# Experts in pairs of 256 tokens with one load of weights, and the leftovers in tiles of 32 tokens that are stationary in column groups

## The chip, the core and the metric

The kernel runs on one core of one Trainium2 chip, everything in float32 as far as the results go. The metric is device time in microseconds of one execution, the median of a few runs. A profiled execution gives the trace; its times are counted from the first instruction.

## What is computed

An attention block turns x and a small state into 8 batches of 544 rows of 512 (4352 tokens). A mixture of experts follows: each token goes to one expert, either the best by its logits or the one of the token before it, and is sent through that expert's two matrices.

```python
for b in range(B):                      # B = 8
    prev_e = -1
    for s in range(S):                  # S = 544
        fresh_e = int(np.argmax(logits[b, s]))
        if s == 0 or local_gate[b, s] < 0.5:
            e = fresh_e
        else:
            e = prev_e if prev_e >= 0 else fresh_e
        prev_e = e
        ...
        h = np.maximum(x[b, s] @ w1[e], 0.0)      # 512 -> 1024
        out[b, s] = p[e] * (h @ w2[e])            # 1024 -> 512
```

There are 8 experts, w1 is 512 x 1024 and w2 1024 x 512 for each, 4.19 MB together.

## The kernel before, in words

**Attention** (classes Attention and Batch) goes over the 8 batches in an order written out by hand and writes the token rows to `rows` in DRAM. Three of its groups of matmuls matter below, since they use parts of TensorE's array: `state_reads` (L404) has a stationary tile of 32 columns in each of four column groups (the trace calls the shape 128*32), `scores` (L336) has 64*32, and `turn` (L391) uses the whole array.

**Routing** (`Routing.route`) sorts the tokens by expert without a loop over tokens. `exc` (L580) has the running count of each expert; from its last column come the number of blocks of 128 of each expert (`nblk`) and where they end (`end`, L588). `at` is the slot of every token: count within the expert plus the expert's first slot (L600 to L611). One comparison and one small matmul (`past`, `be`) tell the expert of every block, which SP needs for the addresses of the weights. `inb`, `bc` and 40 matmuls (L656) then turn slots into lists: `slots.tok` (the token in each place of each block), `slots.row` (the same by quarter rows of 128 numbers) and, later and inside block 0, `slots.prob`. `keep(n)` issues matmuls whose result nobody reads.

**Experts** (`experts`) runs over blocks k of 128 tokens of one expert. `gather(k)` (L724) fetches quarter rows with four indirect DMAs on GpSimd's queue, `turned(k)` (L738) transposes them on VectorE into `x_t`; block 0 is gathered as whole rows (`first`, L719) and transposed on TensorE (L735). `load(k)` (L753) issues the four 1 MB loads of the weights on SP's queue, two halves of w1 into `a`, two of w2 into `c`, each double buffered by the parity of k. In block 0 the halves of `a` are loaded in quarters of 256 KB and pieces of 2 KB (L751). A block is, on TensorE, 32 matmuls with the weights stationary and the 128 tokens moving (L767), and 8 with the tokens' hidden values stationary and 512 columns of w2 moving (L774). ScalarE takes the relu (L769), VectorE scales by the probability (L776), and an indirect DMA scatters to `out` (L777). At its start block k issues the loads and the transposes of block k+1 and the gather of block k+2.

The order of the instructions on each engine is that of the code. SP waits in order: a load stands until the matmuls that read its buffer are done, and the loads behind it stand too. 41 blocks are written down; the first 34 always run, and from then on the code tests the number of blocks (`last`, L797), so that it stops after as many as the counts ask for.

Of the kernel before, what the change touches and what calls it, by code (L numbers as in the profile page):

```python
# [18 lines left out]
P = 128  # L19
# [13 lines left out]
NBLK = NT // P + E - 1  # L33
NJ = NT // P
OFF = 8192
LOW = 32
SQ = 32
CG = 4
NG = COLS // CG
Q = P // SQ  # L40
# [15 lines left out]
):  # L56

# [47 lines left out]
class Slots:  # L105


    def __init__(self, pool):

        self.tok = pool.tile([P, NBLK], I32, name="tok")  # L110

        self.row = pool.tile([P, NBLK, Q], I32, name="row")

        self.prob = pool.tile([P, NBLK], F32, name="prob")

        self.expert = pool.tile([1, 1], I32, name="expert")
        self.again = pool.tile([1, 1], I32, name="again")
        self.experts = pool.tile([1, NBLK - 1], I32, name="experts")
        self.number = pool.tile([1, 1], I32, name="number")
# [326 lines left out]
class Routing:  # L446
# [79 lines left out]
    def route(self, bank, ctx, lt, slots):  # L526
# [31 lines left out]
        for i in range(SC):  # L558
# [22 lines left out]
                                     tot.rearrange("p e c -> p (e c)"), 0.0, Alu.mult, Alu.add)  # L581
        ni = rt.tile([P, E], I32, name="ni")
        nc.vector.tensor_scalar(ni, exc[:, :, COLS], float(P - 1), None, Alu.add)
        nc.vector.tensor_scalar(ni, ni, 7, None, Alu.logical_shift_right)
        nblk = rt.tile([P, E], F32, name="nblk")
        nc.vector.tensor_copy(nblk, ni)
        end = rt.tile([P, 1, E], F32, name="end")
        nc.vector.tensor_tensor_scan(end[:, 0], on[:, 0, 1:E + 1], nblk, 0.0, Alu.mult, Alu.add)  # L588
        first = rt.tile([P, E, 1], F32, name="first")
        firstf = first.rearrange("p e o -> p (e o)")  # L590
        nc.vector.tensor_tensor(firstf, end[:, 0], nblk, op=Alu.subtract)
        nc.vector.tensor_scalar(firstf, firstf, float(P), None, Alu.mult)


        nc.scalar.copy(slots.number, end[0:1, 0, E - 1:E])
        ends = bank(E, 1)
        nc.tensor.matmul(ends, lhsT=end[0:1, 0, :], rhs=one, start=True, stop=True)
        end8 = rt.tile([E, 1], F32, name="end8")
        nc.scalar.copy(end8, ends)
        nc.vector.tensor_tensor(at, exc[:, :, :COLS], pre, op=Alu.add)  # L600
        past = rt.tile([E, NBLK], BF16, name="past")
        nc.vector.tensor_scalar(past, iof[:E, :NBLK], end8, None, Alu.is_ge)
        be = bank(1, NBLK)
        nc.tensor.matmul(be, lhsT=ones[:E - 1, 0:1], rhs=past[:E - 1], start=True, stop=True)
        nc.scalar.copy(slots.expert, be[:, :1])
        others = rt.tile([1, NBLK - 1], F32, name="others")
        nc.scalar.copy(others, be[:, 1:])
        keep(16)

        nc.vector.tensor_tensor(at, at, first.to_broadcast([P, E, COLS]), op=Alu.add)  # L610
# [75 lines left out]
        def probabilities():  # L686
# [10 lines left out]
            for d in (1, 2):  # L697
                nc.vector.tensor_tensor(slots.prob, slots.prob, prob[:, d], op=Alu.add)
            yield
# [4 lines left out]
def experts(ctx, tc, bank, w1, w2, rows, slots, route, out):  # L704
# [7 lines left out]
    xts_ = [fx.tile([P, KT, P], F32, name=f"xt{i}") for i in range(2)]  # L712
    xgs_ = [fx.tile([P, Q, KT, SQ], F32, name=f"xg{i}") for i in range(2)]

    first = fx.tile([P, D], F32, name="first")

    def gather(k):
        if k == 0:
            nc.gpsimd.indirect_dma_start(out=first, out_offset=None,  # L719
                                         in_=rows.rearrange("n q x -> n (q x)"),  # L720
                                         in_offset=bass.IndirectOffsetOnAxis(ap=slots.tok[:, :1], axis=0))
            return
        for i in range(Q):
            nc.gpsimd.indirect_dma_start(out=xgs_[k % 2][:, i].rearrange("p k t -> p (k t)"), out_offset=None,  # L724
                                         in_=rows.rearrange("n q x -> (n q) x"),
                                         in_offset=bass.IndirectOffsetOnAxis(ap=slots.row[:, k, i:i + 1], axis=0))

    def turned(k):
        if k == 0:

            for h, copy in enumerate((nc.vector.tensor_copy, nc.scalar.copy)):
                t = bank(P, KT * P // 2)
                for j in range(KT // 2):
                    q = slice((2 * h + j) * P, (2 * h + j + 1) * P)
                    nc.tensor.transpose(t[:, j * P:j * P + P], first[:, q], route.ident)  # L735
                copy(xts_[0][:, 2 * h:2 * h + 2, :], t.rearrange("p (k t) -> p k t", k=KT // 2))
            return
        nc.vector.transpose(xts_[k % 2].rearrange("p k (i t) -> p k i t", i=Q),  # L738
                            xgs_[k % 2].rearrange("p i k t -> p k i t"))

    def load(k, parts=range(4)):
        expert = slots.experts[0:1, k - 1:k] if k else slots.expert if 0 in parts else slots.again
        e = nc.values_load(expert, engines=[ET.SP], min_val=0, max_val=E - 1,
# [11 lines left out]
    def block(k, ahead=True):  # L755
        a, c, x_t = as_[k % 2], cs_[k % 2], xts_[k % 2]
        if ahead:
            load(k + 1)
            turned(k + 1)
# [77 lines left out]
```

## Time and profile before

| | |
|---|---|
| runs | 670.43 us median of 3 (670.23 to 671.66) |
| the profiled execution, its own time | 669.64 us |
| its span, first to last instruction | 667.8 us |
| attention and routing, to the first expert matmul | 119.3 us |
| expert stage, first matmul to the end of the last | 119.3 to 656.7 us |
| TensorE busy | 630.1 us, 94% of the span |
| mean granted TensorE clock | 0.985 |
| bytes moved by DMA | 206.06 MB |

Where a row of the profile names a group, it has the line, the engine, the operation, what it writes and reads, the shape (128*32 is a part of the array of 128 rows and 32 columns; 128x512 the moving data), the count, busy time and the mean length of one. A matmul's length reaches from its start to the end of its last result, and several are under way at a time; its price in a stream is the distance between starts. A timeline row has the start, the length until the last of the merged instructions ends, and the count; a bracket gives idle time before it and what ended that.

### The profile page before, as it was taken

Reading aid. Unit: us, or ns where it says so; the run is one execution under the profiler, and the core shown is the slowest. Engines: PE = TensorE matmul, PEld = TensorE weight load, DVE = VectorE, ACT = ScalarE, POOL = GpSimd, SP = SyncE. Lnnn points to the kernel's source line nnn. Section 1 sums busy time; section 2 is a strip of 40 time slices with the busy share of each in tenths; the row PEclk is TensorE's granted clock in tenths of the full one; section 3 lists DMA queues with packets and bytes.
Section 4 is the critical chain, followed back from the end, with each engine's and each line's share of the span. In section 5 each row is a group of like instructions: output and inputs, shape, how many; then the busy total and the mean of one; then the engine's idle time right before and its main releaser. Section 6 shows DMA issues by size and latency. Waiting matters only on the chain. (4 is left out here: it accounts for less than half of the span.)

```text
span 667.8 us, 10490 instructions
## 1 busy us (share of the span) xinstructions
PE 630.1 (94%) x4226; PEld 447.2 (67%) x4229; DVE 149.5 (22%) x303; ACT 98.2 (15%) x189; POOL 224.9 (34%) x226
## 2 busy tenths in 40 slices
PE   7688777999999999999999999999999999999993
PEld 2455544867777667776677766777667777667771
DVE  4798978301100001000010000100001100011000
ACT  5455422000010000101001010010100011000110
POOL 4343411522443223432234422344222443223410
PEclk9889997999999999999999999999999999999998
DMA  8969536899999999999999999998999999989910
GB/s 327 373 223 345 213 133 131 325 416 412 348 330 337 323 348 348 337 328 327 350 333 329 337 325 354 338 341 321 322 350 350 338 321 334 335 342 323 336 37 6
DMA packets 41607, 206.06 MB, mean 309 GB/s; under 512 B 9105, under 2 KB 9233, under 8 KB 21330
## 3 DMA queue, kind: packets, MB, share of 16 engines
q1 hardware_dynamic: 33570, 186.18, 75.8%
q0 software_dynamic: 7984, 19.15, 9.1%
q8 instruction: 37, 0.61, 0.4%
q14 instruction: 16, 0.13, 0.1%
HBM read 187.47 MB, written 18.88 MB: 309 GB/s over the span
## 5 line engine op out<-in xcount | busy, mean ns | idle before, releaser
L767 PEld LDWEIGHTS ps<-xt,a 128*128 128x128 f32 x2432 | 277.5, 192 | 18.2 <-issue 17.7
L767 PE MATMUL ps<-xt,a 128*128 128x128 f32 x2432 | 277.8, 275 | 0.3 <-DVE again L688 0.3
L774 PE MATMUL ps<-c,h 128*128 128x512 f32 x608 | 267.2, 592 | 0.0
L774 PEld LDWEIGHTS ps<-c,h 128*128 128x128 f32 x608 | 112.6, 190 | 127.2 <-issue 127.2
L724 POOL DMA_INDIRECT xg<-rows,row x152 | 147.2, 968 | 46.3 <-issue 46.0
L777 POOL DMA_INDIRECT out_dram<-y,tok x38 | 38.5, 1013 | 311.2 <-DVE y L776 311.2
L776 DVE TENSOR_SCALAR y<-ps,prob 128x512 f32<-128x512 f32 x38 | 28.5, 750 | 474.7 <-PE ps L774 474.7
L769 ACT ACTIVATE h<-ps 128x512 f32<-128x512 f32 x76 | 45.4, 597 | 485.6 <-PE ps L767 485.6
L428 PE MATMUL v<-sd,a 128*128 128x265 f32 x128 | 36.9, 428 | 11.6 <-ACT xr L431 8.1
L428 PEld LDWEIGHTS v<-sd,a 128*128 128x128 f32 x128 | 24.2, 203 | 22.9 <-ACT xr L431 13.6
L738 DVE STREAM_TRANSPOSE xt<-xg 128x512 f32<-128x512 f32 x37 | 25.9, 701 | 6.2 <-DMA xg<-rows,row 6.2
L379 POOL TENSOR_TENSOR e<-e,z 128x1024 f32<-128x1024 f32 x8 | 15.3, 1913 | 28.2 <-DVE z L378 28.2
L367 POOL TENSOR_TENSOR e<-e,m 128x1024 f32<-128x1024 f32 x8 | 15.3, 1913 | 16.3 <-DVE m L366 16.3
L336 PE MATMUL s<-x_t,sttc 64*32 64x512 f32 x128 | 11.2, 606 | 2.7 <-issue 2.1
L535 PE MATMUL idle<-place,identb 128*128 128x512 bf16 x42 | 12.4, 451 | 0.6 <-DVE xr L431 0.5
L431 DVE COPY xr<-v 128x530 f32<-128x530 f32 x16 | 10.9, 679 | 4.7 <-PE v L428 4.7
L391 PEld LDWEIGHTS t<-ident,e 128*128 128x128 f32 x64 | 7.5, 149 | 6.4 <-DVE m L366 3.4
L350 ACT ACTIVATE e<-s,nb 128x512 f32<-128x512 f32 x16 | 11.1, 695 | 3.5 <-DVE e L361 1.8
L371 ACT ACTIVATE e<-e 128x1024 f32<-128x1024 f32 x8 | 8.5, 1056 | 17.7 <-POOL e L367 17.7
L346 DVE TENSOR_REDUCE nb<-s 128x1 f32<-128x512 f32 x16 | 10.7, 670 | 0.6 <-PE s L336 0.6
L361 DVE STREAM_TRANSPOSE e<-s 128x512 f32<-128x512 f32 x16 | 10.4, 689 | 2.0 <-PE s L336 1.9
L391 PE MATMUL t<-ident,e 128*128 128x128 f32 x64 | 9.9, 298 | 0.8 <-DVE lt L441 0.7
(149 smaller groups left out, 181.9 us busy)
## 6 DMA issues: line engine op xcount, KB each, us to landing
c<-in_w_dram SPq DMA_DIRECT2D x76, 1024.0 KB
a<-in_w_dram SPq DMA_DIRECT2D x74, 1024.0 KB
x_t<-in_xt_dram SPq DMA_DIRECT2D x16, 512.0 KB
x_n<-in_xn_dram SPq DMA_DIRECT2D x8, 1024.0 KB
rows<-xr SPq DMA_DIRECT2D x8, 1024.0 KB
xg<-rows,row POOLq DMA_INDIRECT x152
a<-in_w_dram SPq DMA_DIRECT2D x8, 256.0 KB
out_dram<-y,tok POOLq DMA_INDIRECT x38
```

The lines of the kernel that those rows point to most:

```text
L367: nc.gpsimd.tensor_tensor(e1, e1, m1.to_broadcast([P, A, N]), op=Alu.subtract)
L379: nc.gpsimd.tensor_tensor(e1, e1, z1.to_broadcast([P, A, N]), op=Alu.mult)
L391: nc.tensor.transpose(self.t[u][:, c * P:c * P + P], self.e2[:, u, c * P:c * P + P], at.ident)
L428: nc.tensor.matmul(v[:, u, :VW], lhsT=self.a[:, u, c * P:c * P + P], rhs=at.sd[:, b, u * VW:(u + 1) * VW], start=True, stop=True)
L535: nc.tensor.matmul(idle, lhsT=identb, rhs=place.rearrange("p k c -> p (k c)"), start=True, stop=True)
L724: nc.gpsimd.indirect_dma_start(out=xgs_[k % 2][:, i].rearrange("p k t -> p (k t)"), out_offset=None, in_=rows.rearrange("n q x -> (n q) x" ...
L738: nc.vector.transpose(xts_[k % 2].rearrange("p k (i t) -> p k i t", i=Q), xgs_[k % 2].rearrange("p i k t -> p k i t"))
L767: nc.tensor.matmul(hps[:, i * P:i * P + P], lhsT=a[half][:, j, i * P:i * P + P], rhs=x_t[:, j, :], start=(j == 0), stop=(j == KT - 1))
L769: nc.scalar.activation(h[:, half * 4:half * 4 + 4, :].rearrange("p m t -> p (m t)"), hps, Act.Relu)
L774: nc.tensor.matmul(yps, lhsT=h[:, m, :], rhs=c[m // 4][:, m % 4, :], start=(m == 0), stop=(m == FK - 1))
L776: nc.vector.tensor_scalar(y, yps, slots.prob[:, k:k + 1], None, Alu.mult)
L777: nc.gpsimd.indirect_dma_start(out=out, out_offset=bass.IndirectOffsetOnAxis(ap=slots.tok[:, k:k + 1], axis=0), in_=y, in_offset=None, bou ...
```

## The change

A unit is now a **pair**: 256 tokens of one expert with one load of its weights (`pair(u)`). An expert has as many pairs as its count holds whole 256s. What is left over goes into **tiles** of 32 tokens (`class Tile`), each with a load of its expert's weights into buffers of their own (`at_`, `ct_`, single).

- In a pair the first product moves 256 columns per matmul; the second is twice the old one, one per 128 tokens. Pair 0 keeps the old shape for the first product.
- In a tile the tokens are stationary. `one()` puts the same 32 columns into each of the four column groups, and each group multiplies another quarter of the hidden values (16 matmuls, 256 columns moving). The relu is taken by ScalarE, and VectorE transposes the result in squares of 32. `two()` does the same with w2 (32 matmuls, 128 columns). The output goes out by quarter rows.
- Tile u is worked in pair u: `one()` behind the pair's first product, `two()` behind its second. When `one()` is issued, SP gets the load of the next tile's w1 (pieces of 2 KB) and GpSimd the tile's gather; behind `two()` come the load of w2 and the tile's transpose.
- 17 pairs and 63 tiles are written down; ten pairs with ten tiles always run, later pairs by a test of their number, later tiles, alone, by a test of theirs.
- The routing counts pairs and tiles, has two ends per expert and a `jump` for the tokens past the last whole pair, and 50 columns of slots instead of 41. The probabilities of the tiles are brought into quarters by four more matmuls (`probq`).

The core of the diff:

```diff
+PAIR = 2 * P
+NP = NT // PAIR
+NPMIN = NP - E * (PAIR - 1) // PAIR
+NTILE = (NT - NPMIN * PAIR) // SQ + E - 1
+NB = NP * 2
+NBLK = NB + (NTILE + Q - 1) // Q
...
+        nc.vector.tensor_copy(ni, count)
+        nc.vector.tensor_scalar(ni, ni, 8, None, Alu.logical_shift_right)
...
+        nc.vector.scalar_tensor_tensor(left, pairs, -float(PAIR), count, Alu.mult, Alu.add)
+        nc.vector.tensor_scalar(ni, left, float(SQ - 1), None, Alu.add)
+        nc.vector.tensor_scalar(ni, ni, 5, None, Alu.logical_shift_right)
...
-        nc.vector.tensor_tensor(at, at, first.to_broadcast([P, E, COLS]), op=Alu.add)
+        nc.vector.tensor_tensor(at, at, each_column(less), op=Alu.add)
+        more = rt.tile([P, E, COLS], F32, name="more")
+        nc.vector.scalar_tensor_tensor(more, at, 0.0, each_column(jump), Alu.is_ge, Alu.mult)
+        nc.vector.tensor_tensor(at, at, each_column(behind), op=Alu.add)
+        nc.vector.tensor_tensor(at, at, more, op=Alu.add)
...
+    class Tile:
...
+        def load(self, of):
+            e = index(slots.experts[0:1, NP - 1 + self.i:NP + self.i])
+            for half in range(2):
+                if of == 0:
+                    w = w1[bass.ds(e, 1), half].rearrange("o p (k f) -> (o p) k f", k=KT)
+                    nc.sync.dma_start(out=at_[:, :, half * F // 2:(half + 1) * F // 2], in_=w)
+                else:
+                    to = ct_[:, half * FK // 2:(half + 1) * FK // 2, :].rearrange("p m d -> p (m d)")
+                    nc.sync.dma_start(out=to, in_=w2[bass.ds(e, 1), half].rearrange("o p x -> (o p) x"))
...
+        def one(self):
+            hps = bank(P, FK * SQ)
+            a = at_.rearrange("p k (m g x) -> p k m g x", g=Q, x=SQ)
+            for j in range(KT):
+                for g in range(Q):
+                    nc.tensor.matmul(hps[SQ * g:SQ * g + SQ, :], lhsT=self.x_t[:, j, :], rhs=a[:, j, :, g],
+                                     start=(j == 0), stop=(j == KT - 1))
...
+        def two(self):
+            yps = bank(P, P)
+            for m in range(FK):
+                for g in range(Q):
+                    nc.tensor.matmul(yps[SQ * g:SQ * g + SQ, :], lhsT=self.h[:, m, :], rhs=ct_[:, m, g * P:g * P + P],
+                                     start=(m == 0), stop=(m == FK - 1))
...
+    def pair(u, ahead=True, tile=None, after=None):
...
+            for n in range(4):
+                hps = bank()
+                for i in range(2):
+                    f = (2 * n + i) % 4 * P
+                    for j in range(KT):
+                        nc.tensor.matmul(hps[:, i * PAIR:(i + 1) * PAIR], lhsT=a[n // 2][:, j, f:f + P],
+                                         rhs=x_t[:, j, :], start=(j == 0), stop=(j == KT - 1))
+                nc.scalar.activation(h[:, 2 * n:2 * n + 2, :].rearrange("p m t -> p (m t)"), hps, Act.Relu)
...
+        if tile:
+            tile.one()
...
+        if after:
+            after.load(0)
+            after.gather()
+        for b in range(2):
+            yps = bank()
+            for m in range(FK):
+                nc.tensor.matmul(yps, lhsT=h[:, m, b * P:b * P + P], rhs=c[m // 4][:, m % 4, :],
+                                 start=(m == 0), stop=(m == FK - 1))
...
+        if tile:
+            tile.two()
+        if after:
+            after.load(1)
+            after.turned()
...
+    gather(0)
+    tiles[0].gather()
+    gather(1)
+    turned(0)
+    tiles[0].turned()
+    next(route.probabilities)
+    load(0, range(2, 4))
+    for of in range(2):
+        tiles[0].load(of)
...
+    for u in range(NPMIN - 1):
+        pair(u, True, tiles[u], tiles[u + 1])
```

How the instructions stand, first on TensorE in the middle of the expert stage, two blocks before (`xt`, `a` and `c` are the buffers named above, the numbers tell the two of each apart):

```order
L767 MATMUL ps<-xt_1471,a_1464 128x128 x16
L767 MATMUL ps<-xt_1471,a_1465 128x128 x16
L774 MATMUL ps<-c_1468,h 128x512 x4
L774 MATMUL ps<-c_1469,h 128x512 x4
L767 MATMUL ps<-xt_1470,a_1462 128x128 x16
L767 MATMUL ps<-xt_1470,a_1463 128x128 x16
L774 MATMUL ps<-c_1466,h 128x512 x4
L774 MATMUL ps<-c_1467,h 128x512 x4
```

and one pair with its tile now (`xtt` and `htt` are the tile's tokens and hidden values, `at` and `ct` its weights):

```order
L875 MATMUL ps<-xt_1494,a_1484 128x256 x16
L875 MATMUL ps<-xt_1494,a_1485 128x256 x16
L838 MATMUL ps<-at,xtt_1498 32x256 x16
L902 MATMUL ps<-c_1488,h 128x512 x4
L902 MATMUL ps<-c_1489,h 128x512 x4
L902 MATMUL ps<-c_1488,h 128x512 x4
L902 MATMUL ps<-c_1489,h 128x512 x4
L850 MATMUL ps<-ct,htt 32x128 x32
```

The 64 matmuls of the two first products became 32 of twice the width, and the tile's two products stand behind the pair's.

SP's queue in the same place, the loads of one pair and of the tile's two halves behind them:

```order
L807 DMA a_1484<-in_w_dram 128x2048
L807 ISA
L807 DMA a_1485<-in_w_dram 128x2048
L807 ISA
L807 DMA c_1488<-in_w_dram 128x2048
L807 ISA
L807 DMA c_1489<-in_w_dram 128x2048
L794 TENSOR_LOAD experts
L827 ISA
L827 DMA at<-in_w_dram 128x4x512
L827 ISA
L827 DMA at<-in_w_dram 128x4x512
```

Before, only loads of `a` and `c` stood in it; now each pair's four are followed by two of the tile's w1 and, behind those, two of its w2.

VectorE in the routing, between the counts and the slots, before:

```order
L588 SCALAR_TENSOR_TENSOR end<-on,nblk 128x8
L591 TENSOR_TENSOR first<-end,nblk 128x8
L592 TENSOR_SCALAR first<-first 128x8
L600 TENSOR_TENSOR at<-exc,ps 128x320
L602 TENSOR_SCALAR past<-iof,end_1311 8x41
L610 TENSOR_TENSOR at<-at,first 128x320
L611 TENSOR_TENSOR at<-at,oh 128x320
```

and now, from the second `end` on:

```order
L607 SCALAR_TENSOR_TENSOR end<-on,tiles 128x8
L618 SCALAR_TENSOR_TENSOR jump<-end,tiles 128x8
L619 SCALAR_TENSOR_TENSOR jump<-jump,behind 128x8
L621 TENSOR_TENSOR at<-exc,ps 128x320
L624 TENSOR_SCALAR past<-iof,end_1321 8x17
L625 TENSOR_SCALAR past<-iof,end_1321 8x63
L637 TENSOR_TENSOR at<-at,less 128x320
L639 SCALAR_TENSOR_TENSOR more<-at,jump 128x320
L640 TENSOR_TENSOR at<-at,behind 128x320
L641 TENSOR_TENSOR at<-at,more 128x320
L642 TENSOR_TENSOR at<-at,oh 128x320
```

Three more operations on 320 columns stand there, and five more on 8 columns above them.

More of the change, by code (lines that the diff above doesn't have):

```diff
@@ L800, in last, with rest @@
         with another.Else():
-            block(k, False)
-    last(NJ - 1)
+            pair(u, False, *with_tile)
+    last(NPMIN - 1, tiles[NPMIN - 1], tiles[NPMIN])
+    def rest(i):
+        with tc.If(more > i):
+            tiles[i].one()
+            if i + 1 < NTILE:
+                tiles[i + 1].load(0)
+                tiles[i + 1].gather()
+            tiles[i].two()
+            if i + 1 < NTILE:
+                tiles[i + 1].load(1)
+                tiles[i + 1].turned()
+                rest(i + 1)
```

223 lines of the change are left out of this document (138 added, 85 removed).

## The prediction

> **What bounds the kernel now.** I read the page first, for the groups that hold TensorE's time. Columns: line, engine, operation, names and shapes, count, then busy us and mean ns of one, then idle time before.
>
> ```profile
> span 667.8 us, 10490 instructions
> ...
> L767 PE MATMUL ps<-xt,a 128*128 128x128 f32 x2432 | 277.8, 275 | 0.3 <-DVE again L688 0.3
> L774 PE MATMUL ps<-c,h 128*128 128x512 f32 x608 | 267.2, 592 | 0.0
> ```
>
> The expert stage is these two lines, and TensorE is never kept waiting in them. 608 records at 16 a block are 38 blocks. (The program has 32 + 8 matmuls in a block, the trace 64 + 16: each is recorded twice.) Next TensorE's timeline over two late blocks; columns are start, length, engine, line, operation, count.
>
> ```profile
> 628.51 7.31 PE L767 MATMUL ps<-xt,a 128*128 128x128 f32 x64
> 635.65 7.03 PE L774 MATMUL ps<-c,h 128*128 128x512 f32 x16
> 642.52 7.31 PE L767 MATMUL ps<-xt,a 128*128 128x128 f32 x64
> ```
>
> From start to start the first product takes 7.14 us, the second 6.87, a block 14.01: 111.6 ns per record of 128 columns, 429.4 ns per record of 512. The line between them has slope (429.4 - 111.6)/384 = 0.828 ns a column and gives 217.5 ns at 256 columns. So wider moving tiles save little; what costs is whole blocks.
>
> Is the DMA close behind? Windows by stage; the last three numbers of a row are granted clock, DMA share and GB/s.
>
> ```profile
> 112.00:113.00 1.00, 0.97 (x13) 0.76 (x10) 0.00 (x0) 0.00 (x0) 0.00 (x0) 1.00 1.10 205
> ...
> 125.00:130.00 5.00, 5.00 (x47) 5.00 (x46) 0.71 (x1) 0.60 (x1) 2.35 (x3) 1.00 1.01 412
> ...
> 300.00:400.00 100.00, 100.00 (x565) 72.07 (x564) 9.58 (x14) 8.96 (x15) 33.79 (x35) 1.00 0.93 334
> ```
>
> In the steady stage it moves 334 GB/s, at full TensorE clock; with free buffers it reaches 412. The SP queue shows why it does not go faster there:
>
> ```profile
> 600.48 7.31 PE L767 MATMUL ps<-xt,a 128*128 128x128 f32 x64
> ...
> 604.25 5.11 SPq L753 DMA_DIRECT2D a<-in_w_dram  x2
> 611.26 3.77 SPq L753 DMA_DIRECT2D c<-in_w_dram  x2
> ```
>
> In the block that starts at 600.48, a is issued from 3.8 us on and c from 10.8 us on, as the matmuls of the block release the buffers one after the other. TensorE bounds, and the DMA follows it.
>
> **Pairs.** Worked through the reference's formulas, the inputs send 1568, 600, 544, 512, 544, 40, 0 and 544 tokens to the eight experts. Rounded up to 128 that is 38 blocks, as the trace has. In whole 256s it is 16 pairs; the rest makes 1+3+1+0+1+2+0+1 = 9 tiles of 32. The program's fixed part runs ten tiles whatever comes (one in each of the first ten pairs), so ten run, the last empty.
>
> Before, the stage holds 38 blocks x 14.01 = 532.4 us of TensorE, plus the probabilities' matmuls (126.53 to 131.16 below), 4.6: together 537. After, pair 0 keeps halves of 128 columns: 2 x 14.01 = 28.0. A later pair has 64 records of 256 columns, 64 x 0.2175 = 13.92 (from 13.74, at half the 512 price, to 14.28, at twice the 128 price; interpolated, since 256 lies between), and the same second product, 2 x 6.87 = 13.74: 27.66, and 15 of them 414.9.
>
> **Tiles.** A tile's first product is 16 matmuls of the program, 32 records of 256 columns, in four column groups; the second 64 records of 128 columns. The nearest rows are in the attention, where L404 uses the same four groups (128*32) and L336 eight groups (64*32); then TensorE returns to the whole array (L391).
>
> ```profile
> 69.32 0.26 PE L404 MATMUL t<-x_n,e 128*32 128x64 f32 x3
> ...
> 69.38 1.06 PE L404 MATMUL t<-x_n,e 128*32 128x64 f32 x61
> 70.36 1.09 PE L336 MATMUL s<-x_t,sttc 64*32 64x512 f32 x16
> 71.39 1.09 PE L391 MATMUL t<-ident,e 128*128 128x128 f32 x8
> ```
> ```profile
> 69.31 0.96 PEld L404 LDWEIGHTS t<-x_n,e 128*32 128x32 f32 x64
> ```
>
> L404: 64 x 64 / 4 = 1024 columns per group, 0.848 us at 0.828, taken 1.04 (69.32 to 70.36). L336: 16 x 512 / 8 = 1024 columns, taken 1.03. The groups do run beside each other, and the excess, 0.18 to 0.19 us, is the same with 64 records and with 16: it belongs to the change of shape of the array, not to a record. The Trainium skill (TensorEngine Tiling (Array Packing), Tiling Modes) says that a change of tiling mode drains TensorE. It gives no price; the trace agrees, at 0.18 us, and that rule is the one that speaks against slipping a small tile into a stream of full matmuls. Each of a tile's products has 2048 columns per group: 1.70 us, and a change in and one out, 0.37: 2.07; a tile 4.14 (so the changes are 7.4 us of the ten tiles). The ends are 3.4, changes free, and 5.0, if moving data in runs of 32 elements or the switch's first weight load cost 0.4 us more per product; the attention's rows are as near as any to this work, so I keep their price. Ten are 41.4. They lie on TensorE's path, in place of the six blocks beyond the 32 that the pairs hold.
>
> **Loads.** In the first ten pairs a step takes 13.92 + 13.74 + 4.14 = 31.8 us and moves two sets of weights, 8.39 MB, and 1.18 MB of gathers and scatters: 9.57 MB, 301 GB/s, below the 334 it sustains now. On SP the tile's first half is queued behind the next pair's four loads and waits for the tile's first product; the pair's loads of the step after stand behind the tile's second half, which waits for its second product. All have 14 us or more to spare: a and c of the next pair are issued as a pair begins, a is wanted 31.8 us later, and with the tile's second half ahead of it that is 4.2 MB, 12.6 us at 334. So the loads hide behind the matmuls. If that cover goes, the price is in the rival below. Pairs 10 to 15 load half as much. On GpSimd a pair has eight gathers and two scatters, as two blocks have, and a tile two more; nobody waits for them within a pair. On DVE a tile's transpose at the end of a pair waits for the tile's gather; behind it stand the next pair's own transposes, wanted 27 us later.
>
> **Before the first block.** DVE's timeline in the routing, then GpSimd's and TensorE's at the start:
>
> ```profile
> 102.37 0.18 DVE L588 TENSOR_TENSOR_SCAN end<-on,nblk 128x8 f32<-128x8 f32 x1
> 102.58 0.17 DVE L591 TENSOR_TENSOR first<-end,nblk 128x8 f32<-128x8 f32 x1
> ...
> 103.41 0.47 DVE L610 TENSOR_TENSOR at<-at,first 128x320 f32<-128x320 f32 x1
> 103.91 0.49 DVE L611 TENSOR_TENSOR at<-at,oh 128x320 f32<-128x320 f32 x1
> ```
> ```profile
> 106.35 1.01 DVE L636 TENSOR_TENSOR inb<-place,blk 128x1640 bf16<-128x1640 bf16 x1
> 107.40 1.01 DVE L638 TENSOR_TENSOR bc<-inb,cols 128x1640 bf16<-128x1640 bf16 x1
> 108.33 0.64 DVE L639 TENSOR_SCALAR bc<-inb,part 128x1640 bf16<-128x1640 bf16 x1
> ```
> ```profile
> 114.41 1.16 POOL L719 DMA_INDIRECT first<-rows,tok  x1 [25.43 <-DVE hw L670]
> 115.88 0.95 POOL L724 DMA_INDIRECT xg<-rows,row  x1 [0.30 <-DVE pr L677]
> ```
> ```profile
> 109.65 3.32 PE L656 MATMUL ps<-bc,inp 128*128 128x82 bf16 x40
> ...
> 118.35 0.63 PE L735 MATMUL ps<-ident,first 128*128 128x128 f32 x4 [1.36 <-DMA first<-rows,tok]
> 119.28 7.41 PE L767 MATMUL ps<-xt,a 128*128 128x128 f32 x64 [0.30 <-DVE again L688]
> 126.53 4.81 PE L656 MATMUL ps<-pb,inp 128*128 128x123 bf16 x40
> 131.16 7.05 PE L774 MATMUL ps<-c,h 128*128 128x512 f32 x16
> ```
>
> All this is serial. Five more steps on 8 columns at 0.21 and a second comparison, 1.25 us; three more on 320 columns at 0.5, 1.5; 50 slots per partition instead of 41 lengthen the three ops from L636 by 22%, 0.58. The 40 matmuls of L656 cost 83 ns a start at 82 columns and 116 at 123, about 0.9 ns a column: 18 more columns are 0.65. The second block's rows are a second gather, 1.47 us after the first, of which some 0.3 lie under the copies: 1.17. Sum 5.2 us (3.5 to 7). The probabilities get 27 columns more, 1.0, and four small matmuls, 0.1. The additions for probq, a transpose per tile and the wait of the first c load for the tile's own gather are hidden: c is wanted 14 us into pair 0, 19 with the probabilities.
>
> **The end.**
>
> ```profile
> 656.80 0.75 DVE L776 TENSOR_SCALAR y<-ps,prob 128x512 f32<-128x512 f32 x1 [13.32 <-PE ps L774]
> 657.83 1.00 POOL L777 DMA_INDIRECT out_dram<-y,tok  x1 [13.06 <-DVE y L776]
> ```
>
> The last scatter is the same, and the 10 us behind it stay. Seven tests of the number of pairs replace five; the last of the old ones stands between the blocks at 628.51 and 642.52, which are 14.01 apart, so tests cost TensorE nothing. The jump over the unused tiles shows nowhere in this trace: 0 to 3 us, and I take 0.5, near the tests, which are its nearest rows.
>
> **The sum.** After: 28.0 + 4.6 + 1.1 + 414.9 + 41.4 = 490.0 against 537.0, so -47.0; start +5.2; end +0.5: -41.3. The profiled execution took 669.64 (span 667.8, and 1.8 around it): 628.3. The median of the runs lies 0.8 above it: **629.1 us**.
>
> **Rivals.** *Weight loads of the column groups do not overlap* (ends slower). Each tile has 96 of them; the attention's cost 110 ns each by the group row
>
> ```profile
> L404 PEld LDWEIGHTS t<-x_n,e 128*32 128x32 f32 x512 | 7.6, 110 | 2.6 <-ACT e L394 2.6
> ```
>
> and if each waited for the matmuls in flight a tile would take 10.6 + 3.4 = 14 us, ten 140, and the kernel 728. It decides from 8.3 us a tile on, where the 41.3 are eaten. The Trainium skill has such a rule (TensorE: Matmul & The Clock Gate, Part 3): loads overlap matmuls in flight only when the row group differs, and here all tiles share their rows. Against it: 64 loads and 64 matmuls of L404 in 1.04 us, where 64 x 110 ns would be 7. 4 in 100.
>
> *Changes of shape cost a whole matmul's latency*: 0.59 us (the mean of L774) instead of 0.18, 40 times: +16, 645. The attention's rows speak against it, but there no full stream of 512 columns comes in between. 8 in 100.
>
> *The DMA bounds the ten-tile steps.* The tile's first half lands in pieces of 2 KB. The only weight load in such pieces, ahead of block 0, ran at 205 GB/s (112 to 113 us) with all queues busy: 2.1 MB then take 10.2 us and the other 7.5 MB at 334 take 22.4, together 32.6, 0.8 over the step; if the rest slows as well, to 310 (my estimate, nearer to 334 than to 205), 34.2. Nine steps by up to 2.4: to 651. For: the pieces. Against: that load filled 32 partitions at a time, this one 128. 9 in 100.
>
> *The split is not as counted*: more leftovers than ten tiles would run alone, each with its 4.2 MB, 10 us and more at 412 GB/s. The 38 blocks of the trace speak against it. One such tile: 641. 1 in 100.
>
> **Chances and range.** The forecast has 75 in 100, with its own range from 618 (changes free -7, start at 3.5 and pairs at their cheapest -4.5) to 641 (tiles at 5.0, +9; end +2.5). The drains and the DMA reach to 651, of which 649 holds the most; a further gain below 618 has 3. Range 618 to 649. The runs before spread by 1.4 us, 0.2%, which is about what can be told from no change: faster 0.95, same 0.01, slower 0.04.
>
> **What would show it.** Pairs 27.7 us apart from start to start without tiles and 31.8 with; tile products 2.1 us each; the first expert matmul at about 124.5; TensorE without a wait for a, c, at or ct; ten tiles, 16 pairs; DMA near 300 GB/s until about 450 us and near 190 after. Wrong would be: steps over 33 us, TensorE waiting for DMA, tile products over 3 us.

## The result, and the profile after

| | before | after |
|---|---|---|
| median of the runs | 670.60 us of 4 (670.23 to 671.66) | 630.61 us of 4 (629.69 to 631.42) |
| the profiled execution, its own time | 669.64 us | 631.42 us |
| its span | 667.8 us | 629.6 us |
| first expert matmul | 119.28 us | 125.93 us |
| last product taken from PSUM | 656.80 us | 614.47 us |
| from there to the end of the span | 11.0 us | 15.1 us |
| bytes moved by DMA | 206.06 MB | 159.35 MB |

The ratio is 0.9401 (95%: 0.9381 to 0.9420). The forecast was 629.1 us, from 618 to 649.

The costliest groups on the page after, in the columns of the prediction's first rows:

```profile
span 629.6 us, 9301 instructions
...
L902 PE MATMUL ps<-c,h 128*128 128x512 f32 x512 | 223.4, 594 | 0.0
L875 PE MATMUL ps<-xt,a 128*128 128x256 f32 x960 | 210.7, 380 | 0.0
...
L850 PE MATMUL ps<-ct,htt 128*32 128x128 f32 x640 | 19.5, 274 | 0.0
L850 PEld LDWEIGHTS ps<-ct,htt 128*32 128x32 f32 x640 | 16.9, 110 | 6.9 <-issue 6.8
```

512 records at 32 a pair are 16 pairs; 640 at 64 a tile are ten tiles. None of these matmuls waits (the last column), so TensorE still bounds the stage. Its timeline, one step with a tile, then a pair without:

```profile
195.36 14.08 PE L875 MATMUL ps<-xt,a 128*128 128x256 f32 x64
209.37 1.93 PE L838 MATMUL ps<-at,xtt 128*32 128x256 f32 x32
211.24 14.00 PE L902 MATMUL ps<-c,h 128*128 128x512 f32 x32
225.17 1.95 PE L850 MATMUL ps<-ct,htt 128*32 128x128 f32 x64
227.05 14.08 PE L875 MATMUL ps<-xt,a 128*128 128x256 f32 x64
...
476.53 13.98 PE L875 MATMUL ps<-xt,a 128*128 128x256 f32 x64
490.35 13.90 PE L902 MATMUL ps<-c,h 128*128 128x512 f32 x32
504.08 13.98 PE L875 MATMUL ps<-xt,a 128*128 128x256 f32 x64
```

From start to start the step is 31.69 us, the pair 27.55, the difference 4.14: the tile's two products at 1.87 and 1.88, and two times 0.2 by which the pair's own products start the next one later (14.01 and 13.93 instead of 13.82 and 13.73). A product of the tile has 1.70 us of columns and costs 2.07, half of the 4.14. The rest, 0.37, is its two changes of shape, one in and one out.

The windows of the steady stage with tiles and of the stage without, up to the last load of weights (length; busy us and count of PE, PEld, DVE, ACT, POOL; clock, DMA share, GB/s):

```profile
300.00:400.00 100.00, 100.00 (x609) 66.03 (x612) 11.11 (x21) 9.30 (x17) 39.07 (x42) 1.00 0.81 309
...
500.00:560.00 60.00, 60.00 (x206) 38.94 (x205) 6.05 (x9) 4.78 (x8) 19.28 (x20) 1.00 0.56 196
```

Before, 0.93 of the DMA was in use; now it is 0.81 and then 0.56. The start, on TensorE:

```profile
113.88 3.91 PE L687 MATMUL ps<-bc,inp 128*128 128x100 bf16 x40 [1.99 <-DVE inp L681]
...
123.73 0.60 PE L790 MATMUL ps<-ident,first 128*128 128x128 f32 x4
124.69 0.63 PE L790 MATMUL ps<-ident,first 128*128 128x128 f32 x4 [0.35 <-DMA first<-rows,tok]
125.93 14.53 PE L886 MATMUL ps<-xt,a 128*128 128x128 f32 x128 [0.61 <-DVE experts L720]
```

And the end, in the order of time: the last product is scaled, scattered, and the program is over.

```profile
614.47 0.75 DVE L906 TENSOR_SCALAR y<-ps,prob 128x512 f32<-128x512 f32 x1 [6.06 <-PE ps L902]
```

Before, the scaling at 656.80 had 11.0 us behind it; here it has 15.1. L952 is the first test of `rest`, the chain of tiles that run alone. GpSimd, which issues the last scatter, is the last engine to reach it. The view of one source line has count, shortest/median/longest in ns, first and last start in us; POOLq is GpSimd's queue of instructions:

```profile
L952 POOLq EVENT_SEMAPHORE  x4: 17/43/43, 620.3 to 620.5; - x4
L952 POOLq COMPARE_BRANCH  x1: 55/55/55, 617.2 to 617.2; - x1
L952 POOLq INC_SWDGE_SEM  x1: 1720/1720/1720, 620.6 to 620.6; - x1
```

No tile runs alone, so the branch at 617.2 jumps over the code of 53 tiles, and the next instruction of GpSimd starts 3.0 us later. Behind the jump come four waits and a semaphore instruction of 1.7 us, which the kernel without the chain, below, doesn't have; they end at 622.3. From 617.2 on that is 5.1 us. The DMA queues in the 3.0 us of the jump (packets, MB, share of the engines):

```profile
...
q14 instruction: 2, 0.02, 1.6%
```

Two packets of instructions are moved in it. The other engines take the same jump earlier: SP at 560.8 us, in 5.3 us, with nothing left to load, so that nobody waits for it. SP's test of the number of pairs (L942), where it jumps over the code of two pairs, costs 0.2.

### The profile page after: what moved, and what is told of

It reads as the page before. It is cut to its first block, busy times and chain, and to the rows that moved or that the text cites. A ratio compares the mean times of both kernels' runs of the same rounds, so it can differ in the third digit from the quotient of the medians.

```text
span 629.6 us, 9301 instructions
## 1 busy us (share of the span) xinstructions
PE 584.8 (93%) x3763; PEld 379.9 (60%) x3763; DVE 155.2 (25%) x335; ACT 95.7 (15%) x190; POOL 217.7 (35%) x218
## 2 busy tenths in 40 slices
DMA packets 43228, 159.35 MB, mean 253 GB/s; under 512 B 8050, under 2 KB 8178, under 8 KB 31395
## 5 line engine op out<-in xcount | busy, mean ns | idle before, releaser
L902 PE MATMUL ps<-c,h 128*128 128x512 f32 x512 | 223.4, 594 | 0.0
L875 PE MATMUL ps<-xt,a 128*128 128x256 f32 x960 | 210.7, 380 | 0.0
L875 PEld LDWEIGHTS ps<-xt,a 128*128 128x128 f32 x960 | 181.6, 190 | 28.4 <-issue 4.4
L902 PEld LDWEIGHTS ps<-c,h 128*128 128x128 f32 x512 | 96.5, 190 | 119.2 <-issue 118.7
L764 POOL DMA_INDIRECT xg<-rows,row x128 | 125.0, 977 | 39.0 <-issue 37.8
L856 POOL DMA_INDIRECT out_dram<-yt,row x10 | 9.8, 981 | 72.7 <-issue 72.7
L387 POOL TENSOR_TENSOR e<-e,z 128x1024 f32<-128x1024 f32 x8 | 15.3, 1913 | 28.2 <-DVE z L386 28.2
L375 POOL TENSOR_TENSOR e<-e,m 128x1024 f32<-128x1024 f32 x8 | 15.3, 1912 | 17.4 <-DVE m L374 17.4
L850 PEld LDWEIGHTS ps<-ct,htt 128*32 128x32 f32 x640 | 16.9, 110 | 6.9 <-issue 6.8
L850 PE MATMUL ps<-ct,htt 128*32 128x128 f32 x640 | 19.5, 274 | 0.0
L838 PE MATMUL ps<-at,xtt 128*32 128x256 f32 x320 | 19.3, 382 | 0.0
L886 PE MATMUL ps<-xt,a 128*128 128x128 f32 x128 | 14.5, 276 | 0.6 <-DVE experts L720 0.6
L886 PEld LDWEIGHTS ps<-xt,a 128*128 128x128 f32 x128 | 14.4, 192 | 0.8 <-DVE experts L720 0.8
```

What stands on the lines that cost most here:

```text
L375: nc.gpsimd.tensor_tensor(e1, e1, m1.to_broadcast([P, A, N]), op=Alu.subtract)
L764: nc.gpsimd.indirect_dma_start(out=to.rearrange("p k t -> p (k t)"), out_offset=None, in_=rows.rearrange("n q x -> (n q) x"), in_offset=ba ...
L838: nc.tensor.matmul(hps[SQ * g:SQ * g + SQ, :], lhsT=self.x_t[:, j, :], rhs=a[:, j, :, g], start=(j == 0), stop=(j == KT - 1))
L850: nc.tensor.matmul(yps[SQ * g:SQ * g + SQ, :], lhsT=self.h[:, m, :], rhs=ct_[:, m, g * P:g * P + P], start=(m == 0), stop=(m == FK - 1))
L875: nc.tensor.matmul(hps[:, i * PAIR:(i + 1) * PAIR], lhsT=a[n // 2][:, j, f:f + P], rhs=x_t[:, j, :], start=(j == 0), stop=(j == KT - 1))
L886: nc.tensor.matmul(hps[:, i * P:i * P + P], lhsT=a[n][:, j, i * P:i * P + P], rhs=x_t[:, j, of], start=(j == 0), stop=(j == KT - 1))
```

## The experiments

Main theory: TensorE's time in the expert stage gives the gain, at the prices of the prediction; of the rest, the jump at the end was sized too small, and the start somewhat too small. Rivals: transfers hold the steps with tiles, or the changes of shape cost more than in the attention, or the time at the end has another cause. The runs were made on four chips; each ratio is against the kernel before on the same chip, where it took 669.87 to 671.12 us. Differences from the result's 630.61 us can cross chips; the first four experiments share one.

**The chain of lone tiles left out.** The part left out is the tiles beyond the tenth, of which these inputs have none.

```diff
-    rest(NPMIN)
```

> Leaves out the chain of lone tiles behind the last pair (it is never entered with these inputs). The changed kernel's span ends 15.2 us after the last matmul, the old one's 11.1. Theory: the 4 us are the jump over that chain, taken only after the last scatter has landed; without it 626.6 us (-4.0) and an end of about 11 us. Rival: the longer end belongs to the pairs' tests or to the larger program as such; then 630.6 and an end of about 15 us.

Measured: 626.12 us (624.59 to 626.67), ratio 0.9331 (0.9317 to 0.9346). Its last scaling:

```profile
613.80 0.75 DVE L906 TENSOR_SCALAR y<-ps,prob 128x512 f32<-128x512 f32 x1 [6.06 <-PE ps L902]
```

The span is 623.8, so 10.0 us follow the scaling instead of 15.1. On the same chip a kernel with the chain (the third experiment) has 15.0 us there and took 629.67. So the extra time at the end is the chain's, 5.1 us by the traces and 3.6 to 4.5 by the medians, and it is paid for code that never runs. Of packets of instructions, the page of the changed kernel counts 35 on one queue and 23 on the other, and this one 33 and 14. The Trainium skill (Runtime: NRT & Kernel Launch, Instruction fetch mechanics) says that a taken branch to code that isn't yet on the engine has to wait for a fetch. The trace agrees, with two packets of instructions in the 3.0 us of GpSimd's jump; the page has no price.

**Two tiles back to back.** The second product of tile u-1 moves from behind pair u-1 to directly ahead of the first product of tile u, so that one change of shape in and one out serve both: 22 changes instead of 40.

```diff
+        if prev:
+            prev.two()
         if tile:
             tile.one()
+        if prev:
+            tile.load(1)
...
-        if tile:
+        if end:
             tile.two()
-        if after:
             after.load(1)
+        if after:
             after.turned()
...
```

> The second product of tile u-1 stands directly ahead of the first product of tile u, between the two products of pair u, so that the array changes its shape 22 times instead of 40. Theory: a change costs 0.18 to 0.19 us, 18 fewer are -3.3 us: 627.3. Rival: the excess over the columns is paid once per product (a first weight load, a last result), whatever stands beside it; then no change, 630.6. Second rival: the second half of a tile's weights, now wanted 14 us earlier after its load is issued, comes late; then slower, by whatever TensorE waits for ct.

Measured: 626.78 us (626.61 to 628.21), ratio 0.9353 (0.9341 to 0.9366). One step on TensorE:

```profile
191.54 13.98 PE L875 MATMUL ps<-xt,a 128*128 128x256 f32 x64
205.45 1.95 PE L850 MATMUL ps<-ct,htt 128*32 128x128 f32 x64
207.22 1.91 PE L838 MATMUL ps<-at,xtt 128*32 128x256 f32 x32
209.06 14.00 PE L906 MATMUL ps<-c,h 128*128 128x512 f32 x32
222.90 13.98 PE L875 MATMUL ps<-xt,a 128*128 128x256 f32 x64
```

The step is 31.36 us instead of 31.69, 0.33 for two changes fewer: 0.17 each, against 0.18 to 0.19 in the attention. Nine such steps are 3.0 us; on the same chip the kernel of the next experiment, with 40 changes, took 2.9 us more. This one leaves nothing out, and it beats both kernels.

**Weights of the tiles loaded once.** What is changed in the computation: every tile after the first uses the first tile's weights.

```diff
         if after:
-            after.load(0)
             after.gather()
...
-            after.load(1)
             after.turned()
```

> Loads weights for the first tile only; all later tiles are multiplied by those, so the leftovers of most experts get the weights of another. 42 MB of loads are gone from the first ten pairs. Theory: those loads lie wholly behind the matmuls; 630.6, steps of 31.7 us as before. Rival: the DMA takes part in setting the step; then the steps fall below 31.7 us and the time by more than 2 us.

Measured: 629.67 us (629.14 to 631.49), ratio 0.9401 (0.9386 to 0.9416). The starts of two neighbouring steps, and the window from 300 to 400 us in this kernel:

```profile
225.32 14.08 PE L875 MATMUL ps<-xt,a 128*128 128x256 f32 x64
...
257.01 14.08 PE L875 MATMUL ps<-xt,a 128*128 128x256 f32 x64
```
```profile
300.00:400.00 100.00, 100.00 (x622) 65.42 (x621) 11.10 (x21) 9.14 (x17) 39.08 (x42) 1.00 0.48 168
```

The DMA moves 168 GB/s instead of 309, and the step is 31.69 us all the same. The tiles' loads are hidden; the rival that they bound the step is out.

**Pairs in halves of 128 columns.** All pairs take the shape that pair 0 has for its first product.

```diff
-        if u:
+        if False:
...
-            next(route.probabilities)
+            if u == 0:
+                next(route.probabilities)
```

> The first product of the pairs moves 128 columns per matmul instead of 256, as in the old kernel and in pair 0; the load of weights per pair stays. Theory: 111.6 ns a record twice against 216 once: 64 x 7 ns = 0.47 us a pair, 15 pairs +7.0: 637.6. Rival: TensorE's weight loads, twice as many, no longer fit beside the matmuls when tiles and pairs alternate; then more than +15.

Measured: 638.54 us (637.16 to 639.82), ratio 0.9525 (0.9509 to 0.9541). A late pair:

```profile
481.11 14.46 PE L886 MATMUL ps<-xt,a 128*128 128x128 f32 x128
495.40 13.90 PE L903 MATMUL ps<-c,h 128*128 128x512 f32 x32
```

The first product is 14.29 us instead of 13.82; 15 x 0.47 = 7.0, and the medians differ by 7.9 from the result and by 8.9 from the third experiment on the same chip. A width of 256 is worth about 1% of the kernel.

**Tokens in the whole array.** The tile's first product has the weights stationary in the whole array and its 32 tokens moving, so that there is no change of shape and no transpose of the hidden values.

```diff
-            for j in range(KT):
-                for g in range(Q):
-                    nc.tensor.matmul(hps[SQ * g:SQ * g + SQ, :], lhsT=self.x_t[:, j, :], rhs=a[:, j, :, g],
+            for m in range(FK):
+                for j in range(KT):
+                    nc.tensor.matmul(hps[:, m * SQ:m * SQ + SQ], lhsT=at_[:, j, m * P:m * P + P], rhs=self.x_t[:, j, :],
                                      start=(j == 0), stop=(j == KT - 1))
...
```

> The tile's first product with the weights stationary in the whole array and the 32 tokens moving, 32 matmuls of the program, 64 records; the second product stays in column groups. Theory of what the column groups are worth: a record then costs what a weight load of the whole array does, about 111 ns as in the old first product: 7.1 us instead of 1.87 plus a change of shape, +5.1 a tile, ten tiles +51: 682, slower than the old kernel. Rival: with 32 columns moving a record is cheaper, some 60 ns; then +19: 650.

Measured: 726.10 us (723.57 to 727.89), ratio 1.0829 (1.0797 to 1.0861). One step, and its first two products as windows:

```profile
187.37 10.81 PE L837 MATMUL ps<-xtt,at 128*128 128x32 f32 x64
197.99 15.35 PE L899 MATMUL ps<-c,h 128*128 128x512 f32 x32
213.27 1.96 PE L847 MATMUL ps<-ct,htt 128*32 128x128 f32 x64
```
```profile
187.30:198.00 10.70, 10.70 (x67) 10.67 (x65) 0.00 (x0) 0.60 (x1) 4.76 (x6) 0.65 0.78 282
198.00:213.30 15.30, 15.30 (x37) 6.54 (x37) 0.75 (x1) 0.38 (x1) 1.02 (x1) 0.91 0.26 86
```

10.6 us for 64 records of 32 columns is 166 ns each, with the weight loads busy throughout, and the granted clock is 0.65 in them. It is still at 0.91 in the pair's product behind them, which takes 15.28 instead of 13.93 in a step of the changed kernel. In the next step the tile's product takes 8.2 us (229.08 to 237.27) and the pair's 16.1 (237.27 to 253.39). So the direction is as expected and the size is not: the low clock costs in both products. The column groups are what makes small tiles worth having: 1.87 us against 8.2 to 10.6.

**An earlier start.** Pair 0 begins on its first 128 tokens; the second 128 are transposed behind the first quarter of the first product.

```diff
-    turned(0)
+    turned(0, (0,))
...
+                    if (b, n) == (0, 0):
+                        turned(0, (1,))
```

> Pair 0 starts on its first 128 tokens as soon as these are transposed; the second 128 are transposed on TensorE behind the first quarter of the pair's first product. Theory: the second gather stood on the path ahead of the first expert matmul, 1.2 us by the sum of the prediction (transposes of the first 128 begin 1.0 to 1.2 us before those of the second in the runs so far); it goes: 629.4, and no wait for the second gather. Rival: the copies behind the inserted transposes hold the next matmuls up by as much, or something else sets the first matmul: 630.6.

Measured: 629.56 us (628.42 to 630.53), ratio 0.9391 (0.9369 to 0.9414). The start, on TensorE:

```profile
123.55 0.60 PE L790 MATMUL ps<-ident,first 128*128 128x128 f32 x4
124.45 3.84 PE L886 MATMUL ps<-xt,a 128*128 128x128 f32 x32 [0.30 <-DVE xt L791]
...
139.28 5.68 PE L687 MATMUL ps<-pb,inp 128*128 128x150 bf16 x40
```

From the first transposes to the probabilities it is 15.73 us; in the changed kernel 140.29 - 123.73 = 16.56. The trace shows 0.8 us of gain; the times (1.05 between medians, on two chips) overlap and settle nothing.

**Nine tiles, the chain ahead of the last fixed pair.** The tenth tile is empty with these inputs. Here nine tiles are fixed, and the chain of the others stands ahead of pair 9, in the hope that the jump lies beside matmuls.

```diff
-    last(NPMIN - 1, tiles[NPMIN - 1], tiles[NPMIN])
...
-    rest(NPMIN)
+    rest(NPMIN - 1)
+    last(NPMIN - 1)
```

> Nine tiles instead of ten run beside the first nine pairs, and the chain of lone tiles, with its test, stands ahead of pair 9 instead of behind the last pair. Theory: the tenth, empty tile cost its 4.14 us, and the jump over the chain, 4 to 5 us at the end, is now taken while TensorE still has matmuls queued: 630.6 - 4.1 - 4.4 = 622. Rival: the jump is paid where it stands, in the middle, by an engine that TensorE then waits for: 626 to 627.

Measured: 630.88 us (630.14 to 631.60), ratio 0.9411 (0.9392 to 0.9430). At the chain, on TensorE:

```profile
422.49 17.08 PE L875 MATMUL ps<-xt,a 128*128 128x256 f32 x64 [6.60 <-DVEq L950]
...
439.40 13.90 PE L902 MATMUL ps<-c,h 128*128 128x512 f32 x32
```

And the window of that product:

```profile
422.40:439.30 16.90, 16.82 (x64) 14.32 (x65) 1.30 (x2) 1.79 (x3) 8.60 (x9) 0.82 0.74 295
```

The hope fell. Every engine takes the jump, and the bracket names VectorE's. The view of the line has it:

```profile
L950 PEldq EVENT_SEMAPHORE  x1: 51/51/51, 418.7 to 418.7; - x1
L950 DVEq COMPARE_BRANCH  x1: 72/72/72, 416.0 to 416.0; - x1
L950 DVEq EVENT_SEMAPHORE  x1: 21/21/21, 422.2 to 422.2; - x1
```

TensorE is through with its own jump at 418.7, but its next product waits for VectorE, which branches at 416.0 and is through at 422.2, after 6.2 us; at the end of the changed kernel the same engine needed 2.8 (614.7 to 617.5). The DMA is 0.98 busy in these 6.2 us and 0.16 in GpSimd's 3.0 at the end; whether that makes the difference was not tried. TensorE stands for 6.60 us in all, and its next product takes 16.91 instead of 13.82 at a granted clock of 0.82. At the end there are 10.2 us behind the last scaling, so 4.9 are saved there; with a tile's 4.14 that is 9.0, and 9.7 are paid in the middle. The rival had the mechanism, at less than half of its price: the chain costs 5 us at the end and 10 in the middle.

**Three edits together**: two tiles back to back, the earlier start, nine tiles with the chain ahead of pair 9 (the edits as above).

> Three edits together: the second product of a tile next to the first of the following one, nine tiles with the chain of lone tiles ahead of pair 9, and the early start of pair 0. If the effects add: 630.6 - 3.0 - 8.5 - 1.2 = 617.9. If the middle jump is paid: 622.

Measured: 626.27 us (625.36 to 628.08), ratio 0.9346 (0.9322 to 0.9370). That is 4 us above even the case in which the middle jump is paid. It has the same hole:

```profile
418.70 15.64 PE L875 MATMUL ps<-xt,a 128*128 128x256 f32 x64 [6.30 <-DVEq L956]
```

**A short chain; a late chain; no chain.** Three kernels on another chip: the changed kernel with a chain of 8 lone tiles instead of 53; the back to back tiles with the earlier start, nine tiles and the chain behind the last pair; and the same with no chain. What they leave out: the first, tiles beyond the eighteenth; the last, tiles beyond the ninth. These inputs have none.

```diff
-            if i + 1 < NTILE:
+            if i < NPMIN + 7:
...
```

> The chain of lone tiles behind the last pair is written down for 8 tiles instead of 53 (tiles 18 and later are left out; none occurs with these inputs). With the full chain the span ends 15.2 us after the last matmul, without it 10.0. Theory: what costs is how far the jump goes, since the jumps over one or two pairs cost nothing; over a seventh of the code the end is near 10 to 12 us, 626 to 628. Rival: any such test behind the last scatter costs its 5 us; 15 us and 630.6.

```diff
-    last(NPMIN - 1, tiles[NPMIN - 1], tiles[NPMIN])
+    last(NPMIN - 1)
...
-    rest(NPMIN)
+    rest(NPMIN - 1)
```

> As the three edits together, but the chain of lone tiles stands behind the last pair again, so that its jump is paid at the end and not in the middle. Theory: 22 changes of shape become 20 (-3.5 against the changed kernel's 40), the tenth tile's 4.1 us go and the start gains 1.0; the jump stays at its 5: 622. Rival: part of the gain of the version with the jump in the middle came from elsewhere; then not below 625.

```diff
-    last(NPMIN - 1, tiles[NPMIN - 1], tiles[NPMIN])
+    last(NPMIN - 1)
...
-    rest(NPMIN)
```

> As before, without the chain: tiles beyond the ninth are left out (none occurs with these inputs). If the effects add: 630.6 - 3.5 - 4.1 - 1.0 - 4.5 = 617.5, the span ending 10 us after the last matmul.

Measured: 639.91 us (638.92 to 643.93), ratio 0.9556 (0.9528 to 0.9584); 638.02 (636.04 to 640.60), 0.9509 (0.9490 to 0.9529); 633.34 (630.53 to 634.29), 0.9447 (0.9431 to 0.9463). All three are far above what was expected, and for a reason that no theory had. In the last one TensorE stands again and again in pair 0, and the waits name no releaser (`issue`: it waited for nothing that the profile shows):

```profile
PE ps L687 <- issue: 5.4, 6, 1.6
...
PE ps L886 <- issue: 3.0, 4, 1.5
```
```profile
137.00:149.00 12.00, 4.04 (x21) 2.71 (x22) 0.00 (x0) 0.88 (x2) 6.82 (x8) 0.67 1.03 397
```

In these 12 us TensorE is busy for 4, while the DMA moves 397 GB/s at a share of 1.03; the mean clock falls to 0.67. The other two have the same hole (5.4 and 5.0 us busy of the 12), so the times say nothing about the chains. The tails still do, read from the last scaling to the end of the span: 12.9 us with 8 lone tiles, 14.6 with the whole chain behind the last pair, 9.8 without. GpSimd's test in the first of them:

```profile
L952 POOLq EVENT_SEMAPHORE  x4: 17/43/43, 629.2 to 629.8; - x4
L952 POOLq COMPARE_BRANCH  x1: 55/55/55, 628.7 to 628.7; - x1
```

Over 8 tiles the jump takes 0.5 us, with no packet of instructions moved in it; over the whole chain it took 3.0, and in the second kernel 2.8 (626.9 to 629.7). What stands behind it takes 2.0 to 2.4 us whatever the length (629.2 to 631.6 here). So both the theory and its rival hold in part: the jump's price goes with the distance, and a test behind the last scatter costs 2.0 to 2.4 us by itself. These are single traces.

**The last one again**, the same kernel on another chip.

> The kernel without the chain once more, unchanged (tiles beyond the ninth are left out; none occurs with these inputs). The three runs before it all lost 10 to 12 us in pair 0, between 137 and 149 us, where TensorE waited for nothing but its own instructions while the DMA moved 390 to 400 GB/s; no earlier run did, and the place lies ahead of the code in which one of them differs from the changed kernel. Theory: that belongs to the chip that ran them, and where it does not show the effects add up to 617.5 us. Rival: it belongs to the programs; then 631 to 634 again.

Measured: **616.87 us** (616.74 to 617.37), ratio 0.9200 (0.9187 to 0.9214), the fastest of the study. Its row of the same window:

```profile
137.00:149.00 12.00, 12.00 (x90) 8.11 (x90) 2.37 (x7) 0.98 (x2) 6.82 (x8) 1.00 1.03 397
```

The same code, the same 397 GB/s, and no hole. The parts add up: 630.61, less 4.5 for the chain, 3.8 for the changes of shape, 1.05 for the start and 4.1 for the tenth tile, is 617.2; by the traces' own differences (5.1, 20 changes at 0.17, 0.8 and 4.1) it is 617.2 as well. Of the 13.8 us between the two spans 9.7 are lost in pair 0, and the other 4 in the tiles' products of later steps, 1.6 of it in waits that again name no releaser. The waits of pair 0 thus do not belong to the program alone; the chip or the session takes part. One could think that instructions came late because their fetches queue beside the loads of weights. The slow trace does not bear that out; its DMA queues from 135 to 155 us are

```profile
q1 hardware_dynamic: 1319, 7.17, 91.1%
q0 software_dynamic: 396, 0.80, 10.9%
```

so no packet of instructions is moved while TensorE stands, and from 148.5 us on TensorE runs without a wait again, also without one. The cause stays open. The kernel before lost nothing on that chip (670.03); the changed kernel did, since the one with the short chain is the same up to the last pair.

## Why the prediction was right, point by point

By its own sum against the spans: predicted -47.0 in the stage, +5.2 at the start, +0.5 at the end; measured -49.0, +6.65 and +4.1. So -38.2 instead of -41.3, 3.1 us short: a stage better by 2.0 hid part of a start and an end that were worse by 1.45 and 3.6. The median came only 1.5 us above the forecast, and that is in part luck: the profiled execution was 0.8 below the median that the forecast started from, and 0.8 above the median after.

- **The stage, 490.0 us:** 488.5 (125.93 to 614.47), against 537.5 before in the same measure (537.0 costed). A pair took 27.55 against 27.66 from the line through 128 and 512 columns: 13.82 us for 64 records is 215.9 ns against 217.5. Fifteen pairs at 0.11 are 1.6 us, the whole difference.
- **A tile, 4.14 us:** 4.14. Taking the price of a change of shape from the attention, as a cost per change and not per record, was the step that held best; the merged tiles took it apart again, 0.17 a change. The rival in which a change lasts a matmul's latency (645) is out. The rule in the Trainium skill (TensorEngine Tiling (Array Packing), Tiling Modes) that a change drains TensorE agrees with these traces, which show its price and not the drain itself.
- **The rival of weight loads that don't overlap (728):** out. Where the Trainium skill (TensorE: Matmul & The Clock Gate, Part 3) has loads overlap only when the row group differs, 64 loads of 110 ns (L850) and their 64 matmuls took 1.88 us here, though all groups share their rows. Here the measurement decides.
- **The loads hidden, DMA near 300 and then 190 GB/s:** 309, and 196 from 500 us to the last load, no wait of TensorE for weights, and no gain when the tiles' loads were taken out. The rival of the DMA (651) is out.
- **Ten tiles, 16 pairs:** as counted.
- **The start, +5.2 us, "the first expert matmul at about 124.5":** +6.65, 125.93, within its 3.5 to 7. Of this 1.07 lies ahead of all that was changed: TensorE's first idle matmul behind the attention, in code that is the same, starts in the two traces, before and after, at

```profile
94.80 2.12 PE L535 MATMUL idle<-place,identb 128*128 128x512 bf16 x8 [0.45 <-DVE xr L431]
```
```profile
95.87 2.12 PE L543 MATMUL idle<-place,identb 128*128 128x512 bf16 x9 [0.45 <-DVE xr L439]
```

 and in the traces of the twelve experiments, which share this code, between 94.11 and 95.92. That is spread of the runs, and 1.07 of the error of 1.45. The routing on DVE gave 113.88 - 109.65 - 1.07 = 3.16 (3.33 costed), the 40 matmuls 0.6 (3.91 against 3.32; costed 0.65 at 0.9 ns a column, though the two prices named beside it, 83 and 116 ns, give 0.8 and thus 0.58), the second gather 1.27 (from the first transposes to the first expert matmul 2.20 against 0.93; 1.17 costed); what I had not counted is some 0.5 by which the idle matmuls of `keep` now end later ahead of the transposes.
- **The end, +0.5 us, "The jump over the unused tiles shows nowhere in this trace":** this is the mis-sized term, +4.1, outside the bound of 3. The sentence on the trace was right: where GpSimd passes the last test before (L797), over the blocks that did not run, it branches at 643.52 and issues again at 643.69. The tests between the pairs were taken as the nearest rows of the new jump; on GpSimd such a test takes 0.2 us, and what it jumps over are a few blocks and not 53 tiles. In their place the runs showed 5.1 us for the chain: 3.0 for GpSimd's jump and 2.1 for what the test puts behind it. The rest of the end, where the sum has "the 10 us behind it stay", became shorter by 1.0 (10.0 without the chain against 11.0 before).

## What to carry to other kernels

Count whole units of work before their shape: the six blocks that no longer run were worth 84 us, 41 of which went back to the tiles, and the wider product was worth 7 to 9. A price that belongs to a switch (shape of the array, a jump) is found by comparing rows with the same work and another number of records, and is paid per switch; so put the odd work back to back. Code that is written down for cases that don't come is not free: look for a jump's price on the engine that passes the test last, not on one that nobody waits for, and try the kernel without the code.

## What the runs showed of the hardware that was not expected

- A test with a jump over 53 unrun tiles costs 5.1 us at the end of the program, 3.0 of it the jump of GpSimd, in which two packets of instructions are moved. Over 8 tiles the jump takes 0.5, over two pairs 0.2 on SP. In the middle it holds TensorE for 6.6 us, by VectorE's jump of 6.2, and the matmuls behind it take 3.1 more, at a clock of 0.82 after the pause.
- With float32 weights in the whole array that change every 32 moving columns, the granted clock was 0.65 though TensorE was never idle, and the next full product took 15.3 to 16.1 us instead of 13.9.
- One and the same program took 633.34 us on one chip and 616.87 on another, the largest piece by TensorE standing in pair 0, beside 397 GB/s of loads, for nothing that the profile shows, where the kernel before was as fast as anywhere. What makes the one chip or session do so stays open.
